# Seven half-height products for pairs of chunks in place of eight, and Silu in place of Sigmoid, in an attention and feed-forward kernel

## Chip, cores, metric

The kernel runs on one core of a Trainium2 chip. The metric is device time in microseconds (us): the median of several executions. A lower time is better. Most executions of one kernel agree within 0.3%.

## The reference, cut

```python
# attention (rwkv5): B, H, S, D = 4, 8, 768, 48; a running state per head
for t in range(S):
    cur = einsum('bhd,bhe->bhde', u * k[t], v[t])
    y[t] = einsum('bhd,bhde->bhe', r[t], state + cur)
    state = w * state + einsum('bhd,bhe->bhde', k[t], v[t])
# feed-forward on the 3072 tokens: d_model 384, d_ff 1536
xn  = x / sqrt(mean(x * x) + 1e-6) * rms_g
g   = xn @ w_gate
out = (g * sigmoid(g) * (xn @ w_val)) @ w_out
```

All is float32 work. The kernel handles the sequence in 12 chunks of 64 steps, 256 tokens each. A chunk's attention yields normalised tokens; two matrices (gate, value) take them to 1536 features ("first layer"), one brings them back ("second layer"). The weights arrive as 64-bit numbers and are rounded on the chip in the first 120 us. Later all weights are read a second time and tested for magnitudes below a limit. That test is called **the check** here; its result only matters for a fallback.

## The kernel before: the parts that matter

```python
def gate_val(blk, nn, nt):                       # nt = 256 or, for a pair of chunks, 512 tokens
    pg = ps_gv.tile(...); pv = ps_gv.tile(...)   # four PSUM banks in turn
    for ps_, wt in ((pg, wg[i]), (pv, wv[i])):
        for cc in range(CC):                     # CC = 3 slices of 128 rows
            nc.tensor.matmul(ps_, wt[:, cc, o * P : (o + 1) * P], xT[:, cc, 0:nt], ...)
    nc.scalar.activation(h, pg, AF.Sigmoid)
    nc.vector.tensor_mul(h, pg, h)
    nc.vector.tensor_mul(h, pv, h)

def checks(n):                                   # 24 of these; "raw" has three buffers
    raw = raws.tile([P, CUT], I64, tag="raw")
    nc.sync.dma_start(out=raw, in_=src[:, k * CUT : (k + 1) * CUT])
    nc.scalar.activation(mag, hi, AF.Abs)
    nc.scalar.activation(mag, mag, AF.Relu, scale=-(2.0**15), bias=1.0, accum_out=seen[:, n : n + 1])

def normalise(s, xT, at):
    nc.tensor.matmul(pm, ones, sq_of[s][:, 0], ...)
    nc.scalar.activation(rms, pm, AF.Sqrt, ...)
    nc.vector.reciprocal(rms, rms)
    ...                                          # three products into xT
blocks = [[3]] + [[s, s + 1] for s in range(4, NS, 2)]   # chunks 0, 1, 2 go alongside the rounding
# ... cut: each block's steps stand beside the attention of the chunks after it
```

The attention of a chunk (`mixing`) interleaves loads (chan, TOK, VS), VectorE products, 32 small scalings on ScalarE and some 200 short matmuls. A scheduler fixes the order of each engine's instructions when the kernel is built.

Of the kernel before, what the change touches and what calls it, by code (L numbers as in the profile page):

```python
# [74 lines left out]
def fast(ctx, tc, chan, tok, vpad, w, u, wgt, wvl, wot, g_cols, out, bad):  # L76
# [7 lines left out]
    wide = wgt.dtype == I64  # L84
    PIECE = NQ * CC * P
    CUT = PIECE // 2

    const = ctx.enter_context(tc.tile_pool(name="const", bufs=1))
    raws = ctx.enter_context(tc.tile_pool(name="raws", bufs=3))
    work = ctx.enter_context(tc.tile_pool(name="work", bufs=2))  # L90
    one = ctx.enter_context(tc.tile_pool(name="one", bufs=1))
    hpool = ctx.enter_context(tc.tile_pool(name="hpool", bufs=NN + 2))
    ps_gv = ctx.enter_context(tc.tile_pool(name="ps_gv", bufs=4, space=PSUM))
    ps_at = ctx.enter_context(tc.tile_pool(name="ps_at", bufs=2, space=PSUM))
    ps_o = ctx.enter_context(tc.tile_pool(name="ps_o", bufs=2, space=PSUM))
# [15 lines left out]
    VS = [c_tile([P, 2, B, VC], f"VS_{i}") for i in range(2)]  # L111
# [12 lines left out]
    def load_v(s):  # L124
        t = VS[s % 2]
        nc.sync.dma_start(out=t[64:128, 0], in_=vpad[s, 64:128])
        nc.sync.dma_start(out=t[0:64, 1], in_=vpad[s, 0:64])
# [7 lines left out]
    for z in range(2):  # L135
# [4 lines left out]
    wg = [c_tile([P, CC, NQ * P], f"wg_{i}") for i in range(WQ)]  # L140
    wv = [c_tile([P, CC, NQ * P], f"wv_{i}") for i in range(WQ)]
    wo = [c_tile([P, NQ, DM], f"wo_{i}") for i in range(WQ)]
    pieces = [
        (dst[i], src[i], k) for i in range(WQ) for dst, src in ((wg, wgt), (wv, wvl), (wo, wot)) for k in range(2)
# [46 lines left out]
    seen = c_tile([P, len(pieces)], "seen")  # L191
    nc.vector.memset(seen, 0.0)

    def checks(n):

        _, src, k = pieces[n]
        raw = raws.tile([P, CUT], I64, name=f"again_{n}", tag="raw")
        nc.sync.dma_start(out=raw, in_=src[:, k * CUT : (k + 1) * CUT])
        hi = raw.bitcast(I32).rearrange("p (n z) -> p n z", z=2)[:, :, 1].bitcast(FP32)
        mag = raws.tile([P, CUT], FP32, name=f"mag_{n}", tag="ulp", bufs=2)  # L200
        nc.scalar.activation(mag, hi, AF.Abs)  # L201
        nc.scalar.activation(mag, mag, AF.Relu, scale=-(2.0**15), bias=1.0, accum_out=seen[:, n : n + 1])

# [25 lines left out]
    for i in range(2):  # L229
        nc.gpsimd.memset(VS[i][0:64, 0], 0.0)  # L230
        nc.gpsimd.memset(VS[i][64:128, 1], 0.0)
# [4 lines left out]
    pw = c_tile([P, HP, L], "pw")  # L236
# [15 lines left out]
    gdup = c_tile([P, HP, 2, L], "gdup")  # L252
    wk = c_tile([P, HP, D], "wk")

    def token_tables():
# [3 lines left out]
        ps = ps_gv.tile([P, HP, P], FP32, name="ps_wk", tag="gv")  # L259
# [24 lines left out]
    kc_of, du_of = {}, {}  # L284

    def prep_r(s):

        kc = kc_of[s] = one.tile([P, B, HP, L], FP32, name=f"kc_{s}", tag="kc")
        table = lambda t: free_dims(t, (0, B), (L, HP), (1, L))
        nc.vector.tensor_mul(ME, CH[:, 0], table(up))  # L290
        nc.scalar.copy(MO[64:128], ME[64:128])
        nc.vector.tensor_mul(kc, CH[:, 1], table(down))  # L292
        if s + 1 < NS:
            load_chan(s + 1)

    def prep_u(s):

        rk = one.tile([P, B, HP, D], FP32, name=f"rk_{s}", tag="rk")
        nc.vector.tensor_mul(rk, TOK[:, 0], TOK[:, 1])
        nc.vector.tensor_mul(rk, rk, free_dims(utab, (0, B), (D, HP), (1, D)))  # L300
        du = work.tile([P, B * HP], FP32, name=f"du_{s}", tag="du")
        nc.vector.tensor_reduce(out=du, in_=rk.rearrange("p b h d -> p (b h) d"), op=ALU.add, axis=AX.X)
        for half in range(2):
            for t, rows in ((ME, slice(64, 128)), (MO, slice(0, 64))):
                if s == 0:
                    nc.vector.tensor_mul(
                        t[rows, 2 * half : 2 * half + 2].rearrange("p b h t -> p (b h) t"),
                        free_dims(dmask[rows], (0, 2 * HP), (1, L)),
                        free_dims(du[rows, 2 * HP * half :], (1, 2 * HP), (0, L)),
                    )  # L310
                    continue
                for b in (2 * half, 2 * half + 1):
                    for p in range(HP):
                        x = b * HP + p
                        nc.scalar.mul(t[rows, b, p, :], dmask[rows], du[rows, x : x + 1])  # L315
# [10 lines left out]

    def scores(s, half):

        kc = kc_of[s]
        pa = ps_at.tile([P, 2, HP, L], FP32, name=f"pa_{s}_{half}", tag="at")  # L330
        for bl in range(2):
            b = 2 * half + bl
            for p in range(HP):
                for rows, to, m in ((slice(0, D), slice(64, 128), ME), (slice(64, 64 + D), slice(0, 64), MO)):
                    nc.tensor.matmul(  # L335
                        pa[to, bl, p, :], kc[rows, b, p, :], m[rows, b, p, :], start=True, stop=True,
                        skip_group_check=True,
                    )
        for to, m in ((slice(64, 128), ME), (slice(0, 64), MO)):
# [4 lines left out]
            )  # L344

    yT_of, sq_of = {}, {}

    def outputs(s, half):

        vs = VS[s % 2]  # L350
        py = ps_at.tile([P, CC, 2 * L], FP32, name=f"py_{s}_{half}", tag="at")
        for bl in range(2):
            b = 2 * half + bl
            cols = slice(bl * L, (bl + 1) * L)
            for i in range(CC):
                at = 3 * D + L * i
                for z, m in ((0, ME), (1, MO)):
                    nc.tensor.matmul(  # L358
                        py[64 * z : 64 * z + 64, i, cols], vs[:, z, b, at : at + L], m[:, b, 3, :],
                        start=True, stop=False, skip_group_check=True,  # L360
                    )
                for z, m in ((0, ME), (1, MO)):
                    nc.tensor.matmul(  # L363
                        py[64 * z : 64 * z + D, i, cols], vs[:, z, b, i * D : (i + 1) * D], m[:, b, i, :],
                        start=False, stop=True, skip_group_check=True,
                    )
        if half == 0:
            yT_of[s] = one.tile([P, CC, B * L], FP32, name=f"yT_{s}", tag="yT")
            sq_of[s] = one.tile([P, CC, B * L], FP32, name=f"sq_{s}", tag="sq")
        cols = slice(half * 2 * L, (half + 1) * 2 * L)  # L370
        nc.scalar.activation(sq_of[s][:, :, cols], py, AF.Square)
        nc.scalar.copy(yT_of[s][:, :, cols], py)
# [5 lines left out]
    def states(s, half):  # L378
# [3 lines left out]
        vs, nx = VS[s % 2], VS[(s + 1) % 2]  # L382
        pu = ps_at.tile([P, 2, HP, D], FP32, name=f"pu_{s}_{half}", tag="at")
        for bl in range(2):
            b = 2 * half + bl
            for p in range(HP):
                for z in range(2):
                    if p < 3:
                        vh = vs[:, z, b, p * D : (p + 1) * D]
                    else:  # L390
                        vh = free_dims(vs[:, z, b, 3 * D + D :], (L, 3), (1, 16))
# [4 lines left out]
        for z in range(2):  # L396
            rows = slice(64 * z, 64 * z + D)
            to = nx[rows, z, 2 * half : 2 * half + 2, :]
# [4 lines left out]
            )  # L403

    def normalise(s, xT, at):
        pm = ps_at.tile([P, B * L], FP32, name=f"pm_{s}", tag="at")
        nc.tensor.matmul(pm, ones, sq_of[s][:, 0], start=True, stop=True)
        rms = one.tile([P, B * L], FP32, name=f"rms_{s}", tag="rms")
        nc.scalar.activation(rms, pm, AF.Sqrt, scale=1.0 / DM, bias=eps)  # L409
        nc.vector.reciprocal(rms, rms)  # L410
        for i in range(CC):
            nc.vector.scalar_tensor_tensor(  # L412
                out=xT[:, i, at : at + B * L], in0=yT_of[s][:, i], scalar=gcol[:, i : i + 1], in1=rms,
                op0=ALU.mult, op1=ALU.mult,
            )

    xTs = {}

    def mixing(s, blk, at):


        def last():
            if at == 0:
                xTs[blk] = work.tile([P, CC, 512], FP32, name=f"xT_{blk}", tag="xT", bufs=3)
            normalise(s, xTs[blk], at)

        def fourth():
            outputs(s, 1)
            states(s, 0)
            states(s, 1)  # L430
            if s + 2 < NS:
                load_v(s + 2)

        return [
            lambda: prep_r(s), lambda: (prep_u(s), prep_k(s)), lambda: scores(s, 0), lambda: scores(s, 1),
# [589 lines left out]
```

## Time and profile before

| | before |
|---|---|
| median | 718.91 us (718.81 to 719.74, 3 runs) |
| profiled span | 717.8 us |
| TensorE busy | 669.5 us, 93% |
| TensorE not busy | 48.3 us |
| mean granted clock | 0.977 |

The prediction below shows the busy table, the slices and the period of two chunks, and how it reads them.

### The profile page before, as it was taken

To read this page: it belongs to the slowest core of one execution; us is meant where nothing else is said; L and a number is where in the kernel's file an instruction comes from. 1 tells how busy PE (TensorE), PEld (TensorE's weight loads), DVE (VectorE), ACT (ScalarE), POOL (GpSimd) and SP (SyncE) were. 2 spreads that over 40 slices of the span, in tenths; PEclk is the share of its full clock that TensorE was granted. 3 is DMA by queue.
4 is the path that set the end of the run, shared out by engine and by line. 5 is a ranking of instruction groups with operands and counts; after the bars stand their busy time and mean duration, and the time that the engine had idled before them with its cause. 6 is when DMAs were issued, how large, how long until landed. Compare 5 with 4: busy or idle time off the path is not lost.

```text
span 717.8 us, 10714 instructions
## 1 busy us (share of the span) xinstructions
PE 669.5 (93%) x4382; PEld 414.0 (58%) x4382; DVE 323.7 (45%) x494; ACT 290.6 (40%) x763; POOL 46.4 (6%) x42
## 2 busy tenths in 40 slices
PE   2378798899999999999999999999999999999995
PEld 2356676677777886445456445456545456544453
DVE  6797978372325674444622444632433420322200
ACT  3365484898127365406326106425205501211000
POOL 7123333000000000000000000000000000000000
PEclk9979799999999999999999999999999999999998
DMA  8856866788015152402204202304200000100001
GB/s 230 226 139 187 258 186 227 271 219 282 1 44 112 41 127 49 102 1 65 63 12 99 62 1 42 86 12 95 67 0 2 0 3 20 23 0 0 1 22 27
DMA packets 17099, 61.05 MB, mean 85 GB/s; under 512 B 3600, under 2 KB 6672, under 8 KB 15888
## 3 DMA queue, kind: packets, MB, share of 16 engines
q1 hardware_dynamic: 17040, 60.27, 31.5%
q8 instruction: 36, 0.59, 0.4%
q14 instruction: 23, 0.19, 0.1%
HBM read 55.54 MB, written 4.72 MB: 84 GB/s over the span
## 4 chain that ended last, share of the span: by engine, by line
PE 80%; DVE 7%; ACT 4%; DMA 3%; issue 3%; POOL 2%; DVEq 0%; POOLq 0%; ACTq 0%
PE pg L450 24%; PE po L468 23%; PE pv L450 23%; PE pa L335 3%; PE py L358 2%; PE py L363 2%; PE pu L392 2%; DMA again<-in_wvl_dram 1%; DVE bits L180 1%; DVE bits L177 1%; DMA chan<-in_chan_dram 1%; DMA again<-in_wgt_dram 1%; ACT mag L201 1%; DVE kc L292 1%; ACT ME L315 1%
## 5 line engine op out<-in xcount | busy, mean ns | idle before, releaser
L450 PE MATMUL pg<-xT,wg 128*128 128x256 f32 (+1 forms) x576 | 209.8, 499 | 8.6 <-DVE xT L412 6.1
L450 PE MATMUL pv<-xT,wv 128*128 128x256 f32 (+1 forms) x576 | 203.6, 490 | 0.1
L468 PE MATMUL po<-wo,h 128*128 128x384 f32 x576 | 194.8, 491 | 5.1 <-DVE h L457 2.6
L450 PEld LDWEIGHTS pv<-xT,wv 128*128 128x128 f32 x576 | 110.7, 193 | 77.7 <-issue 68.9
L450 PEld LDWEIGHTS pg<-xT,wg 128*128 128x128 f32 x576 | 107.8, 193 | 79.6 <-issue 62.2
L468 PEld LDWEIGHTS po<-wo,h 128*128 128x128 f32 x576 | 108.1, 191 | 77.7 <-DVE h L457 5.7
L455 ACT ACTIVATE h<-pg 128x256 f32<-128x256 f32 (+1 forms) x96 | 46.8, 487 | 228.6 <-PE pg L450 228.1
L456 DVE TENSOR_TENSOR h<-pg,h 128x256 f32<-128x256 f32 (+1 forms) x96 | 53.4, 557 | 144.5 <-ACT h L455 144.4
L457 DVE TENSOR_TENSOR h<-pv,h 128x256 f32<-128x256 f32 (+1 forms) x96 | 53.4, 557 | 60.8 <-PE pv L450 59.0
L473 ACT COPY o<-po 128x384 f32<-128x384 f32 x24 | 11.4, 476 | 117.2 <-PE po L468 117.0
L315 ACT ACTIVATE MO<-dmask,du 64x64 f32<-64x64 f32 x176 | 47.7, 338 | 23.4 <-PE py L363 21.0
L315 ACT ACTIVATE ME<-dmask,du 64x64 f32<-64x64 f32 x176 | 44.8, 332 | 0.6
L358 PE MATMUL py<-ME,VS 128*64 128x64 f32 x288 | 37.5, 234 | 6.7 <-DVE MO L340 6.7
L358 PEld LDWEIGHTS py<-ME,VS 128*64 128x64 f32 x288 | 29.6, 145 | 18.9 <-issue 17.3
L410 DVE RECIPROCAL rms<-rms 128x256 f32<-128x256 f32 x12 | 21.0, 1752 | 42.3 <-ACT rms L409 42.3
L358 PE MATMUL py<-MO,VS 128*64 128x64 f32 x288 | 37.4, 233 | 0.0
L335 PEld LDWEIGHTS pa<-ME,kc 48*64 48x64 f32 x384 | 27.1, 148 | 16.6 <-issue 10.6
L290 DVE TENSOR_TENSOR ME<-chan,up 128x1024 f32<-128x1024 f32 x12 | 14.7, 1224 | 47.5 <-PE py L363 46.3
L363 PE MATMUL py<-ME,VS 128*48 128x64 f32 x288 | 36.1, 227 | 0.0
L363 PE MATMUL py<-MO,VS 128*48 128x64 f32 x288 | 36.0, 226 | 0.0
L335 PE MATMUL pa<-ME,kc 48*64 48x64 f32 x384 | 30.1, 236 | 3.6 <-DVE kc L292 3.6
L335 PE MATMUL pa<-MO,kc 48*64 48x64 f32 x384 | 30.0, 236 | 0.0
(81 smaller groups left out, 565.7 us busy)
## 6 DMA issues: line engine op xcount, KB each, us to landing
TOK<-in_tok_dram SPq DMA_DIRECT2D x12, 768.0 KB, 6.9
chan<-in_chan_dram SPq DMA_DIRECT2D x24, 384.0 KB, 6.7
VS<-in_vpad_dram SPq DMA_DIRECT2D x24, 336.0 KB, 5.8
raw<-in_wgt_dram SPq DMA_DIRECT2D x8, 576.0 KB, 4.6
raw<-in_wvl_dram SPq DMA_DIRECT2D x8, 576.0 KB, 4.9
raw<-in_wot_dram SPq DMA_DIRECT2D x8, 576.0 KB, 5.7
again<-in_wgt_dram SPq DMA_DIRECT2D x8, 576.0 KB, 4.9
again<-in_wvl_dram SPq DMA_DIRECT2D x8, 576.0 KB, 4.9
```

Of the source, the lines that this page charges most:

```text
L290: nc.vector.tensor_mul(ME, CH[:, 0], table(up))
L315: nc.scalar.mul(t[rows, b, p, :], dmask[rows], du[rows, x : x + 1])
L335: nc.tensor.matmul(pa[to, bl, p, :], kc[rows, b, p, :], m[rows, b, p, :], start=True, stop=True, skip_group_check=True,)
L358: nc.tensor.matmul(py[64 * z : 64 * z + 64, i, cols], vs[:, z, b, at : at + L], m[:, b, 3, :], start=True, stop=False, skip_group_check=True,)
L363: nc.tensor.matmul(py[64 * z : 64 * z + D, i, cols], vs[:, z, b, i * D : (i + 1) * D], m[:, b, i, :], start=False, stop=True, skip_group_c ...
L392: nc.tensor.matmul(pu[64 * z : 64 * z + D, bl, p, :], KH[:, z, b, p, :], vh, start=True, stop=True, skip_group_check=True,)
L410: nc.vector.reciprocal(rms, rms)
L450: nc.tensor.matmul(ps_, wt[:, cc, o * P : (o + 1) * P], xT[:, cc, 0:nt], start=cc == 0, stop=cc == CC - 1)
L455: nc.scalar.activation(h, pg, AF.Sigmoid)
L456: nc.vector.tensor_mul(h, pg, h)
L457: nc.vector.tensor_mul(h, pv, h)
L468: nc.tensor.matmul(po, hT[blk, nn][:, j * P : (j + 1) * P], wo[i][:, o, :], start=nn == units[0], stop=nn == units[-1])
```

## The change

The intent: a pair of chunks (x, y) times a pair of weight halves takes eight half-height products; with Strassen-like sums of weights and of tokens, seven do. A half-height product uses 64 of TensorE's 128 rows, so gate and value run on two row halves at once. The sums of weights fill the on-chip memory, so the check gets one buffer of half the size. Silu is one ScalarE function in place of Sigmoid and a VectorE product.

```diff
+    def product(ps_, lhs, rhs, start):
+        for cc in range(CC):
+            for z in range(2):                       # two row halves, a PSUM bank each
+                rows = slice(64 * z, 64 * z + 64)
+                nc.tensor.matmul(ps_[:, z, 0:NT], lhs[rows, cc, :], rhs[rows, cc, :], ...)
...
+        def first():
+            product(bank_of("a"), unit(wa[i], o), xa[s], True)
+            nc.scalar.copy(m1, bank["a"][sl])
+        def second():
+            product(bank_of("b"), unit(s2[i], o), t2[s], True)
+            nc.vector.tensor_add(gv[:, :, 1], bank["b"][sl], m1)
+        def third():
+            product(bank_of("c"), unit(s1[i], o), t1[s], True)
+        def fourth():
+            product(bank["b"], unit(s3[i], o), xa[s + 1], False)
+            nc.vector.tensor_add(gv[:, :, 3], bank["b"][sl], m1)
+            nc.vector.tensor_add(gv[:, :, 3], bank["c"][sl], gv[:, :, 3])
+        def fifth():
+            product(bank["a"], unit(wb[i], o), xb[s], False)
+            nc.scalar.activation(gv[:, 0, 0], bank["a"][:, 0, 0:NT], AF.Silu)
+            nc.vector.tensor_mul(h[:, 0], bank["a"][:, 1, 0:NT], gv[:, 0, 0])
+        ...                                          # sixth adds onto b, seventh onto c; two more Silus
...
-        raw = raws.tile([P, CUT], I64, name=f"again_{n}", tag="raw")        # three buffers, 576 KB
+        raw = mine.tile([P, CHECK], I64, name=f"again_{n}", tag="again")    # one buffer, 288 KB
...
-    ps_gv = ctx.enter_context(tc.tile_pool(name="ps_gv", bufs=4, space=PSUM))
+    ps_gv = ctx.enter_context(tc.tile_pool(name="ps_gv", bufs=1, space=PSUM))   # a, b, c: two banks each
...
+    for s in range(FIRST, NS, 2):                    # FIRST = 2: chunks 0, 1 single, then five pairs
+        groups = [f for m in range(NN // 2) for f in group(s, m)]
+        checked = [lambda f=f, x=x: (f(), check() if s > FIRST and x % 2 else None) ...]
+        alongside(checked, near); alongside(outs, far, 1)
```

A "group" is one round of these seven products; a pair has six groups. The rest of the diff is memory and order: single buffers where there were two, loads issued later, `TOK`, `chan` and `VS` overwritten in place, and the steps of the attention cut differently.

## The prediction

> **What bounds the kernel now.** I read the page's busy table and its 40 slices first.
>
> ```profile
> PE 669.5 (93%) x4382; PEld 414.0 (58%) x4382; DVE 323.7 (45%) x494; ACT 290.6 (40%) x763; POOL 46.4 (6%) x42
> ...
> PE   2378798899999999999999999999999999999995
> ...
> PEclk9979799999999999999999999999999999999998
> ```
>
> TensorE (PE) is the bound, and from slice 9 (about 145 us) to the end it never rests, at full clock. No other engine passes 45%. Only the first 120 us, in which the weights are rounded, are limited by something else. Next, the chain that ended last, in order of time, for the period of the main loop and the time of a product:
>
> ```profile
> 291.78 2.57 PE pg L450 x6
> 294.36 2.58 PE pv L450 x6
> ...
> 400.91 2.57 PE pg L450 x6
> ...
> 510.04 2.58 PE pg L450 x6
> ...
> 617.40 2.58 PE pg L450 x6
> ...
> 679.20 30.98 PE po L468 x96
> ```
>
> Two chunks take 109.1 us (291.78 to 400.91 to 510.04); the last two, with no attention beside them, 92.8 us up to the end of L468 at 710.2. Of these 24 x 2.58 = 61.9 us are the first layer, 31.0 the second; so attention costs 109.1 - 92.9 = 16.2 us of TensorE per two chunks. Matmuls of 256 columns take half: 1.29 us for six records (three matmuls, two passes each).
>
> Then the timeline of TensorE inside an attention step, because the change rests on two row halves working at once:
>
> ```profile
> 312.42 0.22 PE L335 MATMUL pa<-ME,kc 48*64 48x64 f32 x1
> 312.43 0.22 PE L335 MATMUL pa<-MO,kc 48*64 48x64 f32 x1
> 312.48 0.22 PE L335 MATMUL pa<-ME,kc 48*64 48x64 f32 x1
> 312.49 0.22 PE L335 MATMUL pa<-MO,kc 48*64 48x64 f32 x1
> ```
>
> ME sits in the lower rows and MO in the upper ones. They start 0.01 us apart and the pair repeats every 0.06 us. At the rate of the wide matmuls (215 ns for 256 columns) one record of 64 columns should take 54 ns, so two do run at once. (These two also use different columns of the array; rows alone are not shown.)
>
> Last, the check that reads all weights a second time (tile again) and the forms that VectorE (DVE) will meet:
>
> ```profile
> L201 ACT ACTIVATE mag<-again x24: 717/732/748, 119.7 to 179.1; 128x576 f32<-128x576 f32 x24
> ...
> DMA to landing us min/median/max: 3.6/4.9/6.2
> ```
> ```profile
> L457 DVE TENSOR_TENSOR h<-pv,h 128x512 f32<-128x512 f32 x48 | 33.2, 692 | 52.0 <-PE pv L450 51.6
> ...
> L410 DVE RECIPROCAL rms<-rms 128x256 f32<-128x256 f32 x12 | 21.0, 1752 | 42.3 <-ACT rms L409 42.3
> ```
>
> The check has three buffers here, its loads overlap, and its 24 steps on ScalarE (ACT) take 2.5 us each without holding TensorE up.
>
> **What the Trainium skill says.** "TensorE: Matmul & The Clock Gate", Part 3, "The mechanism": tiles in different row groups load weights and multiply at the same time. The 0.06 us pairs agree, as far as they go. "TensorEngine Tiling (Array Packing)", "Gotcha 1: PSUM Pressure": row tiles must write different PSUM banks; the change gives each half a bank of its own, no run shows it yet. "DMA: Bandwidth & Descriptors", the anatomy of one DMA: about 2.0 us fixed plus bytes / 436 KB per us. For 576 KB (590,000 bytes) that is 3.35 us; the trace's fastest is 3.6. "ScalarE: Activation LUTs", "What ACT_TABLE_LOAD costs": 1283 ns a load, which the trace shows (1283); Silu needs as many reloads beside Sqrt as Sigmoid did.
>
> **The change part by part.**
>
> (1) Products. Each pair of chunks does 6 groups of 7 products of 1.29 us, 54.2 us, for 61.9: **7.7 us less per pair, 38.7 us for five pairs**, if the halves overlap fully. Chunks 0 and 1 do the eight products.
>
> (2) VectorE. In a group: five 512-wide operations with PSUM (0.69 each), one 512-wide in SBUF (0.69), two of 256 (0.42 to 0.5): 5.1 us per 9.0 us of TensorE. An undisturbed group fits: the tightest wait, the second use of bank b, has 1.29 us for an add of 0.69. Where attention work lies between, it does not. The order of the built program puts, in the fifth group, two TOK products (1.9), the reciprocal (1.75), a reduction (0.94) and the two normalising products (1.9) between two adds: 6.5 us where the sixth product can wait about 3; **I count 3.6 us of stall**. At the start of a pair product two needs t2, which lies behind Sqrt, reciprocal, four products and two subtractions: ready 9.9 us after the last second-layer matmuls before the norm, while TensorE has 5.8 us to do: **4.1 us of stall**. Before, chunks were normalised long ahead. Together 7.7: the pairs with attention win nothing, about 109 us again, of which I add 1.5 for mode switches: 110.5.
>
> (3) The check. SBUF is now full of weight sums, so the check has **one buffer** and 48 steps of 288 KB. A step can load only when the Abs of the step before has read the buffer. Load: 2.0 + 0.295/0.436 = 2.7 us (an estimate from the DMA page; the 3.6 us for twice the bytes agrees). Abs of 288 columns: 0.135 + 0.6/2 = 0.44 (an estimate from 0.73 for 576). Semaphore 0.05. So **3.2 us a step, one after another**. The order of the built program shows where these steps stand on ScalarE: all 48 are pulled forward, between the Sigmoid-like steps h of chunk 1 and the third group of the first pair; for example ten between h_0 and h_5. There TensorE has six units of 2.58 and two outputs of 1.94, 19.4 us, and ten steps need 32. ScalarE goes in order, so Silu waits for loads, the three banks stay full, and TensorE waits. Over the whole stretch: 47 x 3.2 = 150 us, plus what attention work on ScalarE (16 scalings of 0.245, copies, table loads) exceeds a load, about 24 us: **174 us**. TensorE's own work in it: 18 units x 2.58 + 12 outputs x 1.94 + 2.5 attentions x 8.8 + 2.86 groups x 9.0 = 117 us. **So 57 us of new idle time.** The scheduler seems to have counted the row halves as serial and spread the steps over a TensorE time twice too long.
>
> (4) Start. Only chunks 0 and 1 (before: 0, 1 and 2) give TensorE work while the weights are rounded, and all rounding is now ahead of chunk 1's first layer. VectorE has some 96 us of work up to the last piece; before, the last piece came at 118 us. I put the first check at 106 us. TensorE has then done less than before at that time, about 17 us' worth.
>
> (5) Silu in place of Sigmoid and a product: on ScalarE the same, on VectorE 0.42 less per unit. Off the path. Weight sums 8 x 1.35 and token sums are VectorE work inside the stretch of (3), where ScalarE decides.
>
> **Sum.** First check 106 + 174 = 280. Rest of that pair: products left 2.6, py 1.6, three groups 27.1, states and norm 2.5, stall 3.6, second layer 31.0, attention beside it 9.4, stall 4.1: 82, so 362. Three pairs of 110.5 less 2 for the last chunk's missing states: 329, so 691. Last pair: 54.2 + 31.0 + 2.2 for three waits on the one output bank: 87.4, so 779. The tail after the last matmul was 717.8 - 710.2 = 7.6, and the timed run is 1 longer: 787. My working has the stretch of (3) rather at its upper end, so I say **780**.
>
> **The rivals.** *TensorE stays the bound and the saving is real:* 718.9 - 38.7 = 680. For it: 93% busy before. Against: needs both ScalarE and VectorE never to be in the way, and the order shows they are. *Row halves do not overlap:* a product costs 2.58 us, and 258 products (210 in pairs, 48 for chunks 0 and 1) add 333 us to the saving's 680: over 1000. Against: the pairs 0.01 us apart. *Loads of the check are quicker than I think or are kept off the silus* (2.2 us a step): the stretch shrinks to TensorE's 117 plus little, 725. *VectorE alone is the trouble:* without (3) I get 723, and with twice my stalls 755.
>
> **Range and chances.** The step of the check (2.7 to 3.7 us) moves 47 us in all, start and stalls some 15 each way. So **780 us, 8 times in 10 within 742 to 815**. Faster by over 2% asks for rival one or for both stalls and checks to vanish: **0.06**. Within 2%: **0.08**. Slower: **0.86**.
>
> **What would show it.** In the changed profile: matmuls of L439 start in pairs, and six logical ones last 1.29 us (step 1). ScalarE waits for DMA again by about 2 us a step, 48 steps between some 106 and 280 us, with TensorE's slices there at 6 to 7 tenths (step 3). In later pairs TensorE waits for VectorE in one place in the fifth group and one at t2, 3 to 4 us each, period about 110 (step 2). Wrong would make it: checks that land within 2 us; a period of 102 us; or products of 1.5 us and more, which would put it above my range.

## More of the kernel before

One view is added here, because the argument needs it later: the table of windows. Columns are the stretch in us and its length, then busy us (and number of instructions) of TensorE, its weight load, VectorE, ScalarE and GpSimd, the granted clock, the DMA share and GB/s. The first 120 us, before:

```profile
0.00:40.00 40.00, 13.71 (x234) 11.29 (x234) 29.54 (x56) 16.50 (x32) 17.51 (x22) 0.92 0.80 207
40.00:80.00 40.00, 33.74 (x316) 25.70 (x316) 35.07 (x49) 22.21 (x62) 15.41 (x11) 0.91 0.68 188
80.00:120.00 40.00, 35.22 (x181) 27.41 (x182) 35.37 (x53) 22.96 (x57) 12.09 (x9) 0.87 0.70 209
```

TensorE is already busy 82.7 of the first 120 us, although the rounding on VectorE (100 us busy) sets the pace: three chunks give it work that needs only the weights rounded so far.

## The result, and the profile after

| | before | after |
|---|---|---|
| median | 718.86 us (717.35 to 719.74, 4 runs) | 818.08 us (817.47 to 819.38, 4 runs) |
| TensorE busy | 669.5 us | 684.9 us |
| TensorE not busy | 48.3 us | 131.8 us |
| mean granted clock | 0.977 | 0.935 |

The ratio is 1.1385, with a 95% interval of 1.136 to 1.141. A ratio is the mean time of one kernel's fast runs over that of the other's from the same rounds, so it is not quite the ratio of the medians quoted. The output is correct. The kernel is 99 us slower. The direction was predicted; 780 was not, and 818 is outside the range.

The page of the kernel after; the rows are the busy table, TensorE's 40 slices and the granted clock:

```profile
PE 684.9 (84%) x6326; PEld 513.0 (63%) x6326; DVE 407.8 (50%) x575; ACT 354.1 (43%) x955; POOL 47.6 (6%) x40
...
PE   2484875887767778799997999997999999999996
...
PEclk9887898889898889899998999998999999999999
```

Slices are counted from 1 and last 20.4 us. Slices 6 to 17 (102 to 347 us) are at 5 to 8 tenths, where before had nines from slice 9 on. Later two slices fall to 7, the 22nd and the 28th, one in each of two pairs, and the clock falls to 8 tenths in the same slices. Neither VectorE nor ScalarE passes 50%: **neither is the bound by its busy time**.

The chain that ended last shows the products as intended. Start, us, engine and line; x12 is six matmuls of two passes each:

```profile
396.42 1.29 PE c L439 x12
397.72 1.29 PE a L439 x12
```

Twelve half-height records take the 1.29 us that six full-height records of 256 columns took before, so here the two row halves overlap fully, and the rival "row halves do not overlap" is out.

Then the check, first in the same chain, then in the view of its tile and in ScalarE's waits (total us, times, longest):

```profile
110.36 2.67 DMA again<-in_wka_dram
...
113.11 0.47 ACT mag L547
...
113.60 2.67 DMA again<-in_wka_dram
...
116.36 0.48 ACT mag L547
```
```profile
L547 ACT ACTIVATE mag<-again x48: 454/462/481, 113.1 to 304.4; 128x288 f32<-128x288 f32 x48
...
DMA to landing us min/median/max: 2.6/2.7/6.5
```
```profile
ACT mag L547 <- DMA again<-in_wka_dram: 34.3, 14, 6.7
ACT mag L547 <- DMA again<-in_wot_dram: 34.1, 15, 3.1
ACT mag L547 <- DMA again<-in_wkb_dram: 26.3, 13, 2.6
```

One load, one Abs, next load: the step is 3.26 us (113.60 to 116.86). All 48 steps lie between 113.1 and 304.4 us, and ScalarE stood still for 94.7 us of it.

Last, a later pair, in the fifth group (same chain):

```profile
435.32 0.87 DVE KH L310
...
436.21 4.42 DMA TOK<-in_tok_dram
...
440.66 0.97 DVE TOK L300
...
442.61 1.66 DVE rms L418
...
446.95 0.70 DVE gv L589
...
447.70 2.93 PE b L439 x12
450.63 1.65 PE c L439 x12
452.28 1.29 PE a L439 x12
```

VectorE, in order, stands at a product on TOK whose load has not landed, then does the norm of another chunk, and only then the add that frees bank b. TensorE waits 5.8 us. The first product after it takes 2.93 in place of 1.29 us, the second 1.65. The Trainium skill, "TensorE: Matmul & The Clock Gate", Part 1 ("What's actually happening"), states that after an idle window of about 3.4 us the array runs at half clock until it has been busy for such a window. These records agree: half clock after 5.8 us of idling (the granted clock is 0.50 from 447.7 to 450.6 us), worth 2.0 us more. Before its work VectorE had stood idle for 2.09 us, in front of the TOK product at 440.66.

For the accounting below I use one marker that exists in all kernels of the new form: the start of the last second-layer output of a pair (the 24-record po). After: 380.4, 494.2, 609.0, 714.3 and 802.4 us, so pairs of 113.8, 114.8, 105.3 and 88.1 us.

### The profile page after: what moved, and what is told of

It is laid out like the page before. It is cut to its first block, busy times and chain, and to the rows that moved or that the text cites. A ratio compares the mean times of both kernels' runs of the same rounds, so it can differ in the third digit from the quotient of the medians.

```text
span 816.7 us, 14933 instructions
## 1 busy us (share of the span) xinstructions
PE 684.9 (84%) x6326; PEld 513.0 (63%) x6326; DVE 407.8 (50%) x575; ACT 354.1 (43%) x955; POOL 47.6 (6%) x40
## 4 chain that ended last, share of the span: by engine, by line
PE 47%; DMA 19%; DVE 14%; ACT 13%; issue 3%; POOL 2%; SPq 0%; ACTq 0%; DVEq 0%; POOLq 0%
PE po L621 18%; PE b L439 10%; PE a L439 6%; PE c L439 6%; DMA again<-in_wka_dram 5%; DMA again<-in_wot_dram 4%; DMA again<-in_wkb_dram 4%; DMA chan<-in_chan_dram 4%; ACT ME L328 3%; PE pa L337 2%; ACT mag L547 2%; DMA TOK<-in_tok_dram 2%; ACT MO L328 1%; DVE rms L418 1%; PE py L361 1%
## 5 line engine op out<-in xcount | busy, mean ns | idle before, releaser
L439 PE MATMUL b<-t,wb 64*128 64x256 f32 x360 | 49.1, 407 | 19.3 <-DVE gv L589 19.3
L547 ACT ACTIVATE mag<-again 128x288 f32<-128x288 f32 x48 | 22.2, 463 | 94.7 <-DMA again<-in_wka_dram 34.3
L328 ACT ACTIVATE MO<-dmask,du 64x64 f32<-64x64 f32 x176 | 48.3, 338 | 25.8 <-PE py L366 25.2
L439 PE MATMUL gv<-xa,wa 64*128 64x256 f32 x288 | 47.2, 436 | 11.7 <-ACT MO L328 7.5
L439 PE MATMUL c<-t,s 64*128 64x256 f32 x360 | 49.7, 399 | 8.0 <-DVE gv L604 8.0
L439 PEld LDWEIGHTS b<-t,wb 64*128 64x128 f32 x360 | 37.0, 201 | 25.4 <-DVE gv L589 20.9
L439 PE MATMUL b<-xa,wa 64*128 64x256 f32 x360 | 47.9, 398 | 5.2 <-DVE gv L582 5.0
L439 PE MATMUL a<-xa,wa 64*128 64x256 f32 x360 | 49.3, 389 | 3.5 <-DVE h L595 3.5
L439 PE MATMUL b<-t,s 64*128 64x256 f32 x360 | 49.6, 395 | 0.4 <-DVE t L558 0.4
L439 PE MATMUL c<-xb,s 64*128 64x256 f32 x360 | 47.9, 400 | 0.7 <-DVE gv L590 0.5
L439 PEld LDWEIGHTS c<-t,s 64*128 64x128 f32 x360 | 37.7, 197 | 15.1 <-DVE gv L604 9.5
L439 PE MATMUL a<-xb,wb 64*128 64x256 f32 x360 | 45.4, 384 | 0.0
L589 DVE TENSOR_TENSOR gv<-b,m 128x512 f32<-128x512 f32 x30 | 20.7, 692 | 48.4 <-PE b L439 48.3
```

Of the source, the lines that this page charges most:

```text
L328: nc.scalar.mul(t[rows, b, p, :], dmask[rows], du[rows, x : x + 1])
L439: nc.tensor.matmul(ps_[:, z, 0:NT], lhs[rows, cc, :], rhs[rows, cc, :], start=start and cc == 0, stop=cc == CC - 1, skip_group_check=True,)
L589: nc.vector.tensor_add(gv[:, :, 3], bank["b"][sl], m1)
```

## The experiments

Sixteen kernels ran, three rounds each, in four calls; each call has its own runs of the kernel before (medians 720.47, 718.48, 720.53 and 719.09 us). All profiled runs are of the fast state; one execution of the kernel before, in the first call, was slow (894 us) and is left out. An empty field means that the marker was not read there, or does not exist.

| run | us | ratio to before | first pair's last po at | pairs after it |
|---|---|---|---|---|
| after | 818.08 | 1.1385 | 380.4 | 113.8, 114.8, 105.3, 88.1 |
| e1 no check | 757.56 | 1.0542 | 317.5 | 113.7, 115.0, 105.5, 88.1 |
| e2 check loads held | 821.74 | 1.1412 | 324.1 | 127.9, 126.3, 126.3, 108.0 |
| e3 before, one buffer | 723.27 | 1.0059 | | |
| e4 eight products, no check | 769.09 | 1.0681 | 313.2 | 116.8, 116.0, 110.5, 95.7 |
| e5 no check, TOK load held | 787.53 | 1.0952 | | |
| e6 check on GpSimd's queue | 849.72 | 1.1836 | 407.3 | 113.7, 115.1, 106.2, 88.1 |
| e7 check, three buffers | 795.73 | 1.1063 | 357.2 | 115.5, 113.8, 106.1, 88.1 |
| e8 both held | 853.48 | 1.1870 | | |
| e9 Abs held | 789.65 | 1.0986 | 319.6 | 120.0, 121.8, 115.4, 95.5 |
| e10 no check, two TOK buffers | 760.69 | 1.0568 | 315.9 | 114.7, 116.1, 106.0, 88.1 |
| e11 no check, pairs from chunk 4 | 772.03 | 1.0717 | 446.2 (chunks 4, 5) | 115.7, 105.5, 88.1 |
| e12 e10 and e11 together | 770.39 | 1.0712 | 442.0 (chunks 4, 5) | 115.9, 105.6, 87.8 |
| e13 check, loaded once | 778.87 | 1.0829 | 339.5 | 114.8, 113.7, 106.1, 88.1 |
| e14 check, narrow Abs | 811.53 | 1.1277 | 375.9 | 113.5, 115.3, 105.5, 88.1 |
| e15 no check, TOK loaded once | 749.53 | 1.0430 | 316.9 | 113.1, 109.9, 105.2, 88.1 |
| e16 Abs held and narrow | 780.21 | 1.0844 | 320.1 | 120.5, 120.7, 112.9, 92.1 |

### e1: the check taken out

```diff
-    parts = [(src[i], k) for i in range(WQ) for src in (wka, wkb, wot) ...] if wide else []
+    parts = [(src[i], k) for i in range(WQ) for src in (wka, wkb, wot) ...] if False else []
```

> The changed kernel without the second reading of the weights (48 loads of 288 KB and their 96 ScalarE steps are gone; nothing else is). Theory A (the one-buffer check, packed densely on ScalarE, holds TensorE up between 113 and 304 us): ScalarE's 95 us of waiting for those loads goes, the stretch shrinks from 191 us towards TensorE's 117 plus some attention waits, and the kernel takes 735 to 765 us. Theory B (the waits of VectorE and the single buffers of the attention are the loss, the check only fills idle time): 795 to 815 us.

Measured 757.56 us (interval of the ratio 1.0477 to 1.0607). The first pair ends 62.9 us earlier and the later pairs are unchanged within 0.2 us. So **the check costs 60 us, all of it before 380 us**, and some **39 us of loss are left without it**. How TensorE spends the 62.9 us: from 113 us to the marker it is busy 207.9 us and idle 59.5 with the check, 187.0 and 17.5 without. So 42 us are idle time, and 21 are longer records, at a mean granted clock of 0.89 for 0.96.

### e2: the check's loads held back

```diff
-    def check():
+    def check(after):
+        nc.gpsimd.tensor_copy(out=raw.bitcast(FP32)[:, 0:1], in_=after)   # after: a column of h, one group back
```

> The same check with the same single buffer, but each load is made to wait for an h of an earlier group (one column is copied into its buffer by GpSimd first), so that two steps stand in each group of the pairs from chunk 4 on and none before. Theory A: the density was the harm, not the check: within 8 us of the run without a check. Theory C (one buffer costs 3.3 us a step wherever it stands, 48 x 3.3 = 157 us): as slow as the changed kernel, 800 us and more.

Measured 821.74 us: a miss for theory A, and the trace says why. (The time is theory C's, but e3 below speaks against C.) The hold closes a loop; chain of this kernel, in order of time:

```profile
471.74 0.19 POOL again L544
...
471.95 2.69 DMA again<-in_wka_dram
...
475.46 2.81 DMA again<-in_wka_dram
...
479.38 0.28 ACT gv L595
...
485.26 0.19 POOL again L544
```

From one GpSimd copy to the same one a group later are 13.5 us, where a group needs 9.0. Both loads stand, one after the other, in front of the Silu (L595) of the group, whose h starts the next loop. The first pair now ends at 324.1 us, near e1's 317.5, but the later pairs are 11 to 21 us longer than in e1: this moved the wait rather than removing it. Two loads ahead of a Silu in ScalarE's order lengthen this group by 4.5 us.

### e3: the kernel before with a check of one buffer

```diff
-        raw = raws.tile([P, CUT], I64, name=f"again_{n}", tag="raw")
+        raw = raws.tile([P, CUT // 2], I64, name=f"again_{n}", tag="again", bufs=1)    # 48 steps
```

> The kernel before, with its check cut into the same 48 single-buffered steps of 288 KB. Here the scheduler knows TensorE's time rightly and puts about one step beside each unit of 2.6 us or more. Theory A (density): 719 to 735 us. Theory C (one buffer costs 3.3 us a step by itself): 48 x 3.3 = 157 us for what took 60 us, so 770 us and more.

Measured 723.27 us (1.0018 to 1.0101). The view of its check's tile:

```profile
L202 ACT ACTIVATE mag<-again x48: 446/467/487, 116.7 to 333.6; 128x288 f32<-128x288 f32 x48
...
  ACT mag L202: 67.9, 37
```

ScalarE waits 67.9 us for the same 48 loads (the second line), and against the check with three buffers it costs 4 us. So one buffer alone is no great loss. Here the steps are spread over 217 us (116.7 to 333.6) and four first-layer banks stand between TensorE and a late Silu; in the new form one buffer meets crowded steps **and** fewer, dependent banks. Which of these two counts for how much no run separates.

### e4: eight products in pairs, no check

The seven products of a group are replaced by four times (wa, wb), each with its own bank, Silu and product; the weight and token sums go.

> The changed kernel without a check and with eight products in place of seven, on the same row halves: no sums of weights or tokens, no adds on VectorE, one Silu and one product a unit. TensorE has 5 x 7.7 = 38.7 us more to do. If seven products keep their saving: 38 us slower than the run without a check. If the waits on VectorE that seven products bring (some 8 us a pair, 5.8 us of idle time and 2 us at half clock after it) eat it: within 15 us of it.

Measured 769.09 us. Seven products save 3.2, 1.0 and 5.0 us in pairs with attention and 7.5 us in the last pair, which has none: close to the 7.7 counted. In the first pair, which ends 4.4 us later, they save nothing. The whole saves 11.5 of the 38.7 us: the second theory. And the new form (half-height products with single buffers) is slower even with eight products: 116.8 us per pair, where the kernel before takes 109.1.

### e5, e8: the TOK load held back

```diff
-        load_tok(s + 1)
+        # moved behind normalise(s):
+            nc.gpsimd.tensor_copy(out=TOK[64:128, 0, 0, 0, 0:1], in_=xb[s][64:128, 0, 0:1])
+            load_tok(s + 1)
```

> As the kernel without the check, and the load of the next TOK is held (by a one-column GpSimd copy out of the normalised tokens) until the norm of this chunk is done, so that the TOK products stand behind the reciprocal on VectorE. Theory A (the one large wait of TensorE in a pair, 7.1 us for the sums of bank b, is VectorE standing in its order at a TOK product whose load has not landed, and the half clock after it follows from that idle time): the wait falls below 3 us, no product of 2.9 us is left, the pairs with attention fall from 113.7 and 115.0 us to 106 to 110, the whole from 757.6 to 733 to 745 us. Theory B (VectorE has too much work in that group, whatever its order): the wait stays above 5 us and the time within 5 us of 757.6.

Measured 787.53 us, 30 us worse than e1. Chain of e5:

```profile
332.82 4.43 DMA TOK<-in_tok_dram
...
342.09 1.99 ACT ME L329 x8
```

The 32 scalings that need du, which needs TOK, now stand in one block of 7.6 us (342.09 to 349.66) on ScalarE ahead of the Silu of bank a, after a load that starts only behind the norm. TensorE's longest wait for the add fell from 7.1 to 4.0 us, so neither theory came true, but 18.0 us of waits for bank a, eight of them, are new. e8 added this hold to spread check loads:

> The changed kernel with the TOK hold, and each check load held by a GpSimd copy of a column of the group before, two per group, the second marker later than the first, so that in the order of ScalarE one check stands before a group's Silu and one after. Theory A (the miss of the first held version came from two dependent loads standing before one Silu; one alone has 9 us for 3.3 us of load): no wait of ScalarE for a check load above 1 us a group, time 735 to 752. Theory B (any check in the order of ScalarE between a group's adds and its Silu holds TensorE up): groups of 11 us and more, 780 to 830.

Measured 853.48 us: ScalarE waits 122.7 us for check loads, 45 times. It carries the holds of e2 and of e5, and I put the loss down to both; their shares are not told apart.

### e6: the check's loads from GpSimd's queue

```diff
-        nc.sync.dma_start(out=raw, in_=src[:, k * CHECK : (k + 1) * CHECK])
+        nc.gpsimd.dma_start(out=raw, in_=src[:, k * CHECK : (k + 1) * CHECK])
```

> The changed kernel with the check's loads issued from GpSimd in place of SyncE; still one buffer. Theory A (the 37 us by which the stretch of checks exceeds 47 steps of 3.27 us come mostly from loads standing behind one another in SyncE's queue): the stretch falls from 191 to some 174 us, the time from 818 to about 801. Theory B (they come from ScalarE's own attention work and its waits in order): the stretch stays within 5 us of 191 and the time within 6 us of 818.

Measured 849.72 us: neither theory. The check's tile in this kernel, and its landing time:

```profile
L547 ACT ACTIVATE mag<-again x48: 452/462/481, 112.5 to 324.9; 128x288 f32<-128x288 f32 x48
...
DMA to landing us min/median/max: 2.9/3.1/6.8
```

A load takes 0.4 us longer from issue to landing (2.7 to 3.1) and GpSimd needs 0.28 us before it issues, so a step is 3.8 us in place of 3.26. The stretch is 212 us in place of 191: 47 steps by 0.55 us would be 26. The longest load, 6.8 us, is as long as before (6.5), so SyncE's queue was not what delayed the longest loads. By accident this is the experiment "make the step longer", and TensorE pays for it in full: the first pair ends 26.9 us later.

### e7: three buffers, half the size

```diff
-    CHECK = CUT // 2
+    CHECK = CUT // 4
-        raw = mine.tile([P, CHECK], I64, name=f"again_{n}", tag="again")
+        raw = mine.tile([P, CHECK], I64, name=f"again_{n}", tag="again", bufs=3)      # 96 steps
```

> The changed kernel with 96 check steps of 144 KB and three buffers in place of 48 steps of 288 KB and one buffer: the same bytes, the same elements, 96 x 0.3 us of Abs and as much Relu on ScalarE. Theory A (the check costs 60 us because each load must wait for the Abs before it): with three loads in flight a step takes about a third of 2.4 us, the stretch is bound by TensorE again or nearly, time 760 to 785. Theory B (the check costs its ScalarE work and its place in the order, whatever the buffers): 815 or more.

Measured 795.73 us, between the theories. ScalarE's waits for check loads fell from 94.7 to 19.4 us, but only 23 us of the 63 came back: 96 Abs and Relu are 68 us more busy time on ScalarE than no check, all of it between 112.9 and 246.5 us.

### e9, e16: the Abs held back, not its load

```diff
+        nc.gpsimd.tensor_copy(out=mag[:, 0:1], in_=after)      # the Abs writes mag after this
         nc.scalar.activation(mag, hi, AF.Abs)
```

> The changed kernel with all 48 checks and one buffer as they are, but what is held back is the Abs and not its load: a one-column GpSimd copy out of the h of the group before goes into mag ahead of each Abs, two per group. The load can then start as soon as the Abs before it has read the buffer, and has some 4 us. Theory A (the check costs 60 us because the order of ScalarE has a load to wait for directly before the Silus; its own work on ScalarE, about 1 us a step, is free where TensorE is the bound): waits of ScalarE for check loads below 15 us in all (94.6 in the changed kernel), time 757 to 772. Theory B (48 x 1 us of Abs and Relu in ScalarE's order costs TensorE time wherever it stands, as the three-buffer run hints): 785 to 815.

Measured 789.65 us, 28 us less than after, but not 757 to 772: the time is theory B's. Of its waits for check loads 9.1 us are left, and the check's cost at the start is gone (319.6 against 317.5 us), but every later pair is 6 to 10 us longer. ScalarE now stands 42.5 us, in 41 waits, at my marker. ScalarE in the last pair (start, us, line, operation, and in brackets the idle time before it):

```profile
695.08 0.42 ACT L606 ACTIVATE gv<-gv 128x256 f32<-128x256 f32 x1 [1.36 <-DVE gv L605]
696.30 0.47 ACT L548 ACTIVATE mag<-again 128x288 f32<-128x288 f32 x1 [0.81 <-POOL mag L547]
696.80 0.44 ACT L549 ACTIVATE mag<-mag 128x288 f32<-128x288 f32 x1
...
697.24 0.57 ACT L579 COPY m<-a 128x512 f32<-128x512 f32 x1
701.50 0.38 ACT L595 ACTIVATE gv<-a 128x256 f32<-128x256 f32 x1 [3.69 <-PE a L439]
```

The copy m of the next group stands behind the check. It waits 0.81 us for my marker and 0.94 us for the check's work, and the add out of b needs m; TensorE waits for that add five times in this pair, 6.4 us in all. A group takes 10.6 us (690.90 to 701.50 between two Silus of bank a) for 9.06. e16 makes Abs and Relu 2 columns wide:

> The kernel with the Abs held back (789.65 us), with Abs and Relu of 2 columns. Its last pair ran groups of 10.6 us in place of 9.06: in ScalarE's order a check (0.8 us wait for the marker, 1.1 us of work) stands before the copy m of the next group. Theory A (that work is what lengthens the groups): groups of about 9.7 us, 768 to 778. Theory B (the wait for the marker is what lengthens them): groups above 10.2 us, 782 to 790.

Measured 780.21 us and groups of 9.9 us (698.40 to 708.32), between the theories: 0.7 of the 1.5 us were the check's work, the rest the marker and what is left of the operations. TensorE's waits for that add fell with it, from 6.4 to 3.0 us. So **ScalarE has next to no slack in front of the copy m**: of some 1.8 us there (0.81 + 0.94) 1.5 are paid. Right behind that copy it stands idle for 3.69 us of the same group, waiting for TensorE (the last line shown).

### e13, e14: loads and work of the check apart

e13 loads the buffer once and keeps all 48 Abs and Relu; e14 keeps all 48 loads and looks at 2 columns:

```diff
-        raw = mine.tile(...); nc.sync.dma_start(...)     # e13: for n == 0 only
-        nc.scalar.activation(mag, hi, AF.Abs)
+        nc.scalar.activation(mag[:, 0:2], hi[:, 0:2], AF.Abs)      # e14, the Relu likewise
```

> The changed kernel with the check's buffer loaded once: all 48 Abs and Relu stay, on the same data, nothing is read a second time (the output is right, the check is not done). This is ScalarE's own work of the check, 48 x 1.1 us, without one load to wait for; the built order still pulls all 48 ahead, up to 13 of them between two Silus of chunk 1. Theory A (nearly all of the 60 us are the loads): 757 to 775. Theory B (the work alone, pulled ahead into the order of ScalarE, holds the first layer's banks up, as the runs with three buffers and with held Abs hint): 785 to 800, with the rest, some 25 us, being the loads.

> The opposite: all 48 loads into one buffer stay, but Abs and Relu look at 2 columns of 288 (the check is then incomplete, the output right). A step falls from 3.27 to about 2.9 us of load, semaphore and two short operations, so the chain of loads is nearly as long. Theory A (the chain of loads is what counts): the stretch loses 48 x 0.35 = 17 us and no more, 795 to 810. Theory B (ScalarE's work is the larger part): 770 to 788.

Measured 778.87 and 811.53 us. Over e1 that is 21 us for the work without loads and 54 us for the loads without work, 60 for both (they overlap). The loads are the larger part, as predicted, though 811.53 lies just above e14's range. e13 falls between its two theories: the work alone still costs 21 us. In its trace up to seven steps stand between two Silus (125.87 to 133.67 us; I had read up to 13 in the built order). e7, with twice as many steps of half the width and short waits for loads, costs 40 us over e1 at the first pair's end (357.2 for 317.5), e13 22.

### e10, e15: why a pair without the check takes 113.7 us

e10 gives TOK two buffers (and h six in place of seven):

> As the kernel without the check, with two TOK buffers in place of one (and six h buffers in place of seven, to make room); every engine's order in the pairs is the same. Theory A (the long wait in the fifth group and the half clock after it come from the TOK load not having landed): the wait of TensorE for the add into bank b falls from 7.1 to about 3 to 4 us at most, products after it take at most 1.7 us, the pairs that began at 317.5 and 431.2 us take 106 to 110 us in place of 113.7 and 115.0, the whole 735 to 748 us for 757.6. Theory B (VectorE's own work in that group is the wait): 752 to 760.

Measured 760.69 us; no gain, and no test either. VectorE's order of this kernel, in the fifth group (brackets: idle before it, and what ended it):

```profile
373.25 0.69 DVE L587 TENSOR_TENSOR gv<-b,m 128x512 f32<-128x512 f32 x1 [0.18 <-PE pm L420]
376.05 0.96 DVE L301 TENSOR_TENSOR TOK<-TOK 128x768 f32<-128x768 f32 x1 [2.11 <-DMA TOK<-in_tok_dram]
...
382.35 0.69 DVE L594 TENSOR_TENSOR gv<-b,m 128x512 f32<-128x512 f32 x1
```

With a free buffer the scheduler pulled the products of one chunk further ahead, to the same place behind a load that had just started. The wait stays. e15 takes the load itself away (wrong output: later chunks use stale TOK data):

```diff
-        load_tok(s + 1)
```

> As the kernel without the check, with TOK loaded for chunk 0 only (wrong result on purpose: later chunks use stale data). In the built order the TOK products then stand in the fourth group, ahead of the KH products, and only the reciprocal and the two normalising products (3.7 us) stand between two adds of the fifth group. Theory A (the stall in the fifth group is the TOK load and products standing between the adds): the largest wait of TensorE for the add into bank b falls from 7.1 to under 3 us, no product of 2.9 us is left, pairs with attention 105 to 109 us in place of 113.7 and 115.0, the whole 733 to 745. Theory B (the stall only moves to another add): 752 to 760.

Measured 749.53 us, 8 less than e1 and between the theories; A asked for 13 to 25. TensorE's waits for this add, first e1, then e15:

```profile
PE b L439 <- DVE gv L589: 19.9, 4, 7.1
```
```profile
PE b L438 <- DVE gv L588: 16.1, 7, 4.2
```

The longest falls from 7.1 to 4.2 us. Pair by pair, the long wait is 4.2 us in place of 7.1 (first pair), 4.2 in place of 5.8 and 2.3 in place of 6.0. No product of 2.9 us is left; after the two waits of 4.2 us the products take 1.9 and 2.1 us, at a granted clock of 0.79 and 0.71. But the scheduler built another order here too. VectorE before the add of one of the 4.2 us:

```profile
367.36 0.95 DVE L303 TENSOR_REDUCE du<-TOK 128x16 f32<-128x768 f32 x1 [3.57 <-ACT MO L327]
...
370.22 0.68 DVE L588 TENSOR_TENSOR gv<-b,m 128x512 f32<-128x512 f32 x1
```

VectorE now stands 3.57 us idle at a reduction that waits for ScalarE's scalings, so what is left is a new wait and not the rest of the old one. e15 shows that the long waits shrink without the load; it does not tell the load from VectorE's work. The trace of e1 gives an estimate: before the add that ends the 5.8 us, VectorE stands idle 2.07 us for TOK (377.38) and then works without a pause to 384.36. Without that idle time the wait would be some 3.7 us, so about 2 us are the load and the rest is work: two TOK products, reciprocal, reduction and norm between two adds.

### e11, e12: pairs from chunk 4 on

Chunks 2 and 3 do the eight products one chunk at a time, in the order of the kernel before, to give TensorE work while the weights are rounded; e12 has two TOK buffers as well.

> As the kernel without the check, but chunks 2 and 3 do the eight products one chunk at a time, in the order of the kernel before, and seven products begin at chunk 4. Theory A (about 34 us are lost up to the end of chunk 3, because TensorE has only chunks 0 and 1 to work on while the weights are rounded and then waits for two norms): chunk 4's first product at 290 to 305 us (in the kernel without the check the pair 4, 5 begins at about 325), 720 to 737 us in all. Theory B (the loss at the start is the rounding's own place on VectorE, not the chunks that TensorE has): within 8 us of 757.6.

> Both of these together, and the norm's scratch kept in the square's buffer to save 1 KB. If the two losses are independent, the times add up: 757.6 less about 28 (start) less about 14 (three pairs by 4 to 6 us) makes 705 to 725 us, at or just under the kernel before, still without the check. If they hide behind the same thing (VectorE), 730 or more.

Measured 772.03 and 770.39 us. e11 misses both its theories (14 us above 757.6); e12 is on the side of "730 or more". Chunk 4's first product came at 333.6 us, later than in e1 (325.4, but for two records), and much later than in the kernel before (291.8). Up to there TensorE is busy 275.2 us, before 251.0, and idle 58.4 for 40.8. So 24 of the 42 us are longer records and 18 are idle time. Single chunks in the half-height form are slower than before (three units and two outputs take 12.4 us: 2 x 2.13 + 5.38 + 2.79; before 11.6: 6 x 1.29 + 3.87): each of the four pieces is 0.2 us longer than its records at full rate. **The loss at the start was not given back by any experiment, and its cause is only partly shown.**

## Why the prediction was wrong, by its steps

**Step 1, the products: right.** 1.29 us for six half-height matmuls, all through. In e4 against e1 a pair without attention saves 7.5 us; 7.7 was counted.

**Step 3, the check: right in mechanism, and in size with luck.** 57 us of new idle time were predicted; taking the check out gave 60.5 (818.1 less 757.6). The step was 3.26 us for 3.2, and all 48 stood where the built order had them. (The estimate of the load, 2.7 us, came true, but the skill's page gives that sum for loads that GpSimd issues, and SyncE issues these; see the end.) Two misses cancelled: the stretch was longer, 191 us for 174, since what else stood in it came to 38 us and not 24 (191 less 47 x 3.26); and what TensorE needs for the same work without the check was longer too, some 128 us for 117. Nor is it all idle time, as said: of e1's 62.9 us 42 are idle and 21 longer records. The loads are the larger part of the cost (e13, e14), one buffer alone is not enough for it (e3), and a longer step is paid in full (e6).

**The step that failed is the sum without the check, "without (3) I get 723", above all its start.** Measured, 757.6 us. Of these 34 us:

- *Step 4, the start, and the first pair, about 20.* The first check came at 113 us for 106 (+7). In the kernel after, VectorE had been busy 91 of the first 109.5 us, so its work, counted as 96 us, was not too small; its idle time was. TensorE's time for the stretch without the check was taken as its own work at full rate, 117 us; e1 needs an estimated 128 (317.5, less 113, less the 76 us that lie between the last check and the marker after: 380.4 less 304.4) (+11). In these 128 us (113 to 241.5) e1's TensorE is busy 119.2 and idle 9.3: the work was counted rightly, the idle time left out. The rest of the first pair took 84 for 82 us (+2). The first three windows of e1 show where it begins:

```profile
0.00:40.00 40.00, 11.85 (x230) 10.52 (x230) 31.86 (x61) 19.04 (x51) 19.47 (x21) 0.92 0.83 222
40.00:80.00 40.00, 27.26 (x196) 19.11 (x197) 37.79 (x44) 21.21 (x42) 18.90 (x13) 0.78 0.69 218
80.00:120.00 40.00, 33.86 (x342) 25.13 (x344) 31.23 (x37) 24.12 (x65) 9.51 (x6) 0.87 0.39 109
```

TensorE is busy 73.0 of the first 120 us, before 82.7. By the end of chunk 3 (325.5 us in e1, 291.8 before) it had been busy 261 us for 251 and idle 65 for 41. Of the 24 us of extra idle time 10 lie in the first 120 us and 14 after. Its two largest waits from 120 to 325.4 us in e1:

```profile
PE b L439 <- DVE gv L589: 7.1, 1, 7.1
PE pu L395 <- ACT VS L403: 5.3, 3, 2.8
```

The first is the fifth group's wait of the first pair, the second ScalarE's copies into VS; the start of the pair, which waits for two norms, shows 0.6 us. I had written of 17 us less work done at 106 us (measured, after against before: 10, or 61.6 us busy for 71.3), but never charged the idle time between 120 us and the first pair.

- *Step 2, the pairs, about 5.* Period 113.7 and 115.0 for 110.5, but 105.5 for the third. The composition was wrong more than the sum. In e1 a pair of 113.7 us is the 101.4 counted (54.2 products, 31.0 second layer, 16.2 attention), 7.0 TensorE not busy, 2.3 half clock, 1.4 more second layer (32.4, since its parts of 12 records take 4.07 us, not 3.87), and, by difference, 1.6 for the rest. The stall of the fifth group was 5.8 us plus 2.0 to 2.3 for the clock, not 3.6: I counted VectorE's work, which by the estimate above is some 3.7 us of it, but neither the TOK load that it stands at nor the half clock. The stall at t2, predicted 4.1 us, is under 0.5: the last output of the second layer covers 7.94 us, where I had counted half of that. That the sum came near is luck: one stall was too small, the other too large.

- *The last pair and the tail, about 2*: 88.2 us for 87.4, and 9.7 for 8.6.

- *My rounding, 7.* The sum was 787; I said 780 because I thought the stretch was at its upper end. It was not.

Half clock was not in the prediction at all, although the skill's page was named in it for another section.

**The rivals.** "VectorE alone is the trouble: 755 with twice my stalls" comes close to e1's 757.6, but for another reason: the stalls came to some 8.6 us a pair (5.8 + 2.3 + under 0.5) for 7.7, and it was the start that was late.

**Why no version of the new form beats the kernel before.** The best is e15 with 749.5 us, without a check and with a wrong result. e1's TensorE is busy 665.2 us, only 4.3 less than before: of the 38.7 us saved, 34 go back, by difference, into longer records of TensorE. Half clock, changes between the forms of matmul and the half-height single chunks are seen above; their shares were not measured apart. Its idle time is 90.9 us for 48.3.

**What stays open.** Why TensorE is idle 10 us more in the first 120 us: no experiment changed this alone, and e11, which was meant to, changed too much at once. Whether an order that puts the Abs behind the copy m, where ScalarE idles 3.69 us in a group, without a marker, would make the check free. And what the check costs in the kernel before: no run takes it out there, so e1, without a check, is compared with a kernel that has one.

## What to carry to other kernels

Fewer products help only where the path that frees their banks has room: here, with seven products in three dependent banks, TensorE waited for ScalarE's and VectorE's order, not for their busy time (43 and 50%), and removed work came back as waits and longer records. When a change shrinks buffers, ask where the scheduler will put the work that used to hide: going from three buffers to one cost 4 us in the kernel before, while in the new form, with its crowded order, the check with one buffer cost 60 us over no check and 22 over three quarter-size buffers. And check a sum by taking out the suspected term; the term may be right and the rest wrong.

## What the Trainium skill lacked or had wrong

- "TensorEngine Tiling (Array Packing)", "Key Properties", says that changing the tiling mode drains TensorE, without a figure. Here a six-matmul product right after attention matmuls takes 1.50 us for 1.29 (e1, 342.37), and twelve records of the second layer after them 4.07 for 3.87. We read this as about 0.2 us a switch; no run changes the mode alone.
- "ScalarE: Activation LUTs", "What ACT_TABLE_LOAD costs", adds about 1380 ns of drain to 1283 ns of load for each switch of table set. The load is 1.28 us here; no drain shows on either side (the twelve loads before Sqrt in the kernel after: 0.2 us of idle time before them in all, 0.1 behind). ScalarE of e10:

```profile
372.64 0.59 ACT L583 COPY m<-a 128x512 f32<-128x512 f32 x1
373.24 1.28 ACT L422 ACT_TABLE_LOAD   x1
374.54 0.47 ACT L422 ACTIVATE rms<-pm,eps 128x256 f32<-128x256 f32 x1
```

- "DMA: Bandwidth & Descriptors", "Anatomy of one DMA", gives 2.0 us plus bytes / 436e3 for loads issued by GpSimd. For 288 KB that is 2.68 us: the loads from SyncE measured 2.7 (median), those from GpSimd 3.1. For 144 KB (2.34 us) SyncE's measured 2.3. The fit held for SyncE's loads and was 0.4 us short for GpSimd's.
- "TensorE: Matmul & The Clock Gate", Part 1: nothing wrong. Waits of 5.8 us and more for the add were followed by 2.93 us for the first product; after waits of 4.2 us in e15 it took 1.9 and 2.1 us, so half clock held for a part of it only. The page's line that ScalarE and VectorE take their queues strictly in order ("Architectural detail") agrees with the waits shown above.
